# Batch 0's first key-value products in 32-column tiles, and one ScalarE instruction moved ahead of two copies

## The chip, the core and the metric

The kernel runs on one core of a Trainium2 chip. The metric is the device time of the whole program in microseconds (us); the figure quoted is the median of three runs. The engines are called PE (TensorE, matrix products), PEld (its weight loads), DVE (VectorE), ACT (ScalarE), POOL (GpSimd) and SP (SyncE, which here only issues DMA transfers). A line such as L444 is line 444 of the kernel. A "start" is counted in us from the beginning of the profiled span.

## What is computed

Attention with polynomial features, followed by a two-layer network with an exact GELU. Per batch (4) and head (4), with 1088 tokens of 32 numbers and two sketches S1, S2 of 8 rows each:

```
phi(x)[i, j] = (S1 x)[i] * (S2 x)[j]                 # 64 features a token
kv  = sum over tokens of phi(k) v^T ;  z = sum of phi(k)
x   = (phi(q) kv) / (phi(q) z + 1e-6)                # heads side by side: 4352 x 128
out = gelu(x @ w_in) @ w_out                         # 128 -> 2048 -> 128
```

The inputs moe_w_in and moe_w_out come as 64-bit floats, so each of their pieces is landed as pairs of 32-bit words and rounded to float32 by ACT, DVE and POOL before PE may use it.

## The kernel before

The bulk of the time is the two-layer network: for each chunk of 512 tokens, 16 products with w_in (`hidden`, L739), a GELU on ACT (L746) and products with w_out (L825, L876). The attention of batches 1 to 3 is woven into it. Batch 0 cannot be woven into anything: its attention stands at the head of the program, and the network begins when its first x is there. The change lies in that head, between 8.4 and 16 us of the span.

Every engine executes its instructions in the order of the program text (the last lines of the kernel, L1239 to L1245, fix that order by hand), and an instruction that waits holds up all behind it on its engine. The order of the text around the change:

- **PE**: the turn of the remainder keys (`key_turn_rem`, L347); `kv_first(kv_bank, 0, range(JC))`, the products of even heads for the first four token groups (L444); the sketches of the remainder keys (`key_features_rem`, L420); `kv_first(kv_bank, 0, range(JC, J))`, the other four groups; `kv_first(kv_bank, 1, parts=2)`, the odd heads; `kv_first_rem`, the remainder tokens (L450); the turn of the second query chunk (`query_turn(1)`, L347); the numerators of chunk 0 (`numerators_by_token`, L684, first into a bank called h_ps, then into one called o_ps); the first factor of chunk 1's query features (`expand_products(1, (0,))`, L569); the turn of the first half of x (L720); the second factor (L569); the turn of the second half (L712); the first hidden product in pieces (`first_hidden`, L755); then `hidden` (L739).
- **ACT**: the copy of the turned remainder keys (kT_rem, L349); the widening of v (L359); the copy of the remainder sketches (a_rem, L428); two copies for the query features of chunk 0 (A_sb, L575); the two copies of kv and z into kz_apart (L950), which is the moving operand of the numerators; the low words of w_in's first piece (`low_words`, L269); the exponents of that piece (L293); the copy of the turned second query chunk (qT, L954); one denominator (L705); the low words of w_in's second piece; half of x (L721); that piece's exponents (L293); a quarter of x (L714).
- **DVE**: two products of query features (q_pT, L580); the mantissas of w_in's first piece (bits_m, L301), which read the low words; the denominators and the division of the first half of x (L695, L697, L699); the signs (L306); the second half (L697, L699); the exponent and mantissa fields of w_in's second piece (L282, L287); its mantissas (L301); a quarter of x (L714).
- **POOL**: the features of the remainder keys (k_p_rem, L429), which `kv_first_rem` reads; two one-element fills that gate the loads of w_out on SP; the product that finishes w_in's first piece (L311).

A key-value product takes 128 tokens as its contraction, a token group's features as weights (64 of one head, or 32 with `parts=2`) and 33 columns of v with its column of ones as the moving operand. Each product is two records on PE. With 64 weights it takes a 128x64 tile of the array (written 128\*64 in the profile); with `parts=2` it takes a 128x32 tile (128\*32), and there are twice as many of them. Before the change the even heads use 128x64 tiles and the odd heads 128x32 tiles. The remainder products (L450), the sketches (L420) and the numerators (L684) are in 128x64 tiles throughout.

Of the kernel before, what the change touches and what calls it, by code (L numbers as in the profile page):

```python
# [16 lines left out]
def kernel(  # L17
# [26 lines left out]
    J = S // 128  # L44
    MAIN = J * 128
    REM = S - MAIN
    JC = 4
# [29 lines left out]
    def hidden_bank():  # L77
        return hps.tile([128, CW], FP, name="h_ps")

    def out_bank():  # L80
        return ops.tile([128, CW], FP, name="o_ps")
# [259 lines left out]
    def transposed(ps, name, srcs, copy, midway=lambda: None):  # L341

        n = len(srcs) * 128
        for i, s in enumerate(srcs):
            if 2 * i == len(srcs):
                midway()
            pe.transpose(ps[:, i * 128:(i + 1) * 128], in_=s, identity=ident)  # L347
        t = att.tile([128, n], FP, name=name, bufs=1 if name == "kT_rem" else 2)
        copy(out=t, in_=ps[:, :n])  # L349
        return t  # L350
# [10 lines left out]
    def widen_v_rem(b, copy=by_pool):  # L361
        if b:
            pool.memset(v_rem_aug[b], 0.0)
        rows = slice(b // 2 * REM, (b // 2 + 1) * REM)
        copy(out=v_rem_aug[b][rows, :, 0:D], in_=rem["v"][rows, b % 2])
# [51 lines left out]
    def key_features_rem(pair, ps, by_dve=True):  # L417

        for rows in (slice(0, 64), slice(64, 128)) if pair == 0 else (slice(0, 128),):
            pe.matmul(ps[rows, 384:448], lhsT=kT["rem"][:, rows], rhs=S12.rearrange("p h r -> p (h r)"), start=True, stop=True)  # L420
        k_p_rem[pair] = big.tile([128, H, R, R], FP, name=f"k_p_rem{pair}")
        ab = ps[:, 384:448].rearrange("p (h r) -> p h r", r=2 * R)
        a = att.tile([128, H, 2 * R], FP, name="a_rem")
        if by_dve:
            act.copy(out=a[:, :, 0:R], in_=ab[:, :, 0:R])
            dve.tensor_mul(**spread(k_p_rem[pair], a[:, :, 0:R], ab[:, :, R:2 * R]))
        else:
            act.copy(out=a, in_=ab)  # L428
            pool.tensor_mul(**spread(k_p_rem[pair], a[:, :, 0:R], a[:, :, R:2 * R]))  # L429
# [3 lines left out]
    def flat(features):  # L433
        return features.rearrange("p i j -> p (i j)")

    def kv_first(ps, r, tokens=range(J), parts=1):

        step = F // parts
        for i in tokens:
            for c in range(NP):  # L440
                for part in range(parts):
                    rows = slice(c * F + part * step, c * F + (part + 1) * step)
                    features = flat(k_p[0, r][:, i // JC, c * JC + i % JC])
                    pe.matmul(ps[rows, r * 2 * D:r * 2 * D + C], lhsT=features[:, part * step:(part + 1) * step],  # L444
                              rhs=v_aug[r][:, c, i, :C], start=(r == 0 and i == 0), stop=False, skip_group_check=True)
# [93 lines left out]
    def query_turn(n, copy=by_act):  # L539


        if n == 1:
            turned = transposed(hidden_bank(), "qT", [q_sb[1][:, h].rearrange("p j d -> p (j d)") for h in range(H)], copy)
            qT[n] = turned.rearrange("p (h j t) -> p h j t", h=H, j=JC)
            return
        qT[n] = att.tile([128, H, width[n] // 128, D], FP, name="qT" if n < NMAIN else "qT_rem")
        if n == 0:
            for c in range(NP):
                heads = slice(2 * c, 2 * c + 2)
                dve.transpose(out=qT[n][:, heads].rearrange("p h j t -> p h (j t)"),  # L550
                              in_=q_sb[n][:, heads].rearrange("p h j d -> p h (j d)"))
            return
        dve.transpose(out=qT[n].rearrange("p h j t -> p (h j t)"),
                      in_=q_sb[n].rearrange("p h j d -> p (h j d)") if n < NMAIN else q_rem.rearrange("p s b n d -> p (s b n d)"))
# [18 lines left out]
    def expand_copy(n, i):  # L573
        A[i] = att.tile([128, 2, CW // 2], FP, name="A_sb")
        act.copy(out=A[i][:, :, :width[n] // 2], in_=B_of[n, i][:, :, :width[n] // 2])  # L575
# [352 lines left out]
    kv_bank = out_bank()  # L928
# [1 line left out]
    widen_v(1, by_act, slice(0, JC))  # L930
    widen_v(1, by_pool, slice(JC, J))
    widen_v_rem(0, by_dve)
    kv_first(kv_bank, 0, range(JC))
    key_features_rem(0, second[1], by_dve=False)
    expand_copy(0, 0)
    w_in = [Rounding(w) for w in w_in_sb[:2]]
    w_in[0].fields()
    kv_first(kv_bank, 0, range(JC, J))
    expand_copy(0, 1)
    for i in range(2):  # L940
        expand_multiply(0, i)
# [3 lines left out]
    load_rest()  # L945
    late = []
    query_turn(1, lambda **a: late.append(a))
    for c in range(NP):
        rows = slice(c * F, (c + 1) * F)
        act.copy(out=kz_apart[rows, :, c], in_=kv_bank[rows, :128].rearrange("f (r x) -> f r x", r=2)[:, :, :C])  # L950
    w_in[0].low_words()
    w_in[0].exponents()
    w_in[0].mantissas()
    by_act(**late.pop())  # L954
# [1 line left out]
    parts = [range(2), range(2, JC)]  # L956
# [319 lines left out]
```

## Time and profile before

| what | value |
|---|---|
| median of three runs | 259.12 us (258.75 to 259.46) |
| the profiled execution: its own time | 259.21 us |
| the profiled execution: its span, first to last instruction | 257.4 us |
| busy share of PE, PEld, DVE, ACT, POOL | 98%, 52%, 59%, 45%, 64% |
| granted clock of TensorE | 1.0 |
| key-value products of batch 0 (L444) | 96 PE records: 32 in 128x64 tiles, 64 in 128x32 tiles, from 8.4 to 10.2 us |

The page of the profile gives busy time by engine, a picture of the span in 40 slices, and the chain of work that ended last. The timeline gives, in order of time, when a group of instructions starts, from its first start to its last end. PE's records overlap one another, so a group's length is not its cost: what counts is the distance from one start to the next.

### The profile page before, as it was taken

Reading aid. Unit: us, or ns where it says so; the run is one execution under the profiler, and the core shown is the slowest. Engines: PE = TensorE matmul, PEld = TensorE weight load, DVE = VectorE, ACT = ScalarE, POOL = GpSimd, SP = SyncE. Lnnn points to the kernel's source line nnn. Section 1 sums busy time; section 2 is a strip of 40 time slices with the busy share of each in tenths; the row PEclk is TensorE's granted clock in tenths of the full one; section 3 lists DMA queues with packets and bytes.
Section 4 is the critical chain, followed back from the end, with each engine's and each line's share of the span. In section 5 each row is a group of like instructions: output and inputs, shape, how many; then the busy total and the mean of one; then the engine's idle time right before and its main releaser. Section 6 shows DMA issues by size and latency. Waiting matters only on the chain.

```text
span 257.4 us, 5633 instructions
## 1 busy us (share of the span) xinstructions
PE 253.1 (98%) x2265; PEld 133.3 (52%) x2265; DVE 151.1 (59%) x314; ACT 115.1 (45%) x222; POOL 165.4 (64%) x175
## 2 busy tenths in 40 slices
PE   8999999999999999999999999999999999999995
PEld 4756444355444545444444455455544444445794
DVE  3886878969698987580178976399307000700330
ACT  3785767533535333533335332623444334433442
POOL 3414007799968788587758775787758777877300
PEclk9999999999999999999999999999999999999999
DMA  6699568610000101102000002000200200020020
GB/s 209 207 287 314 148 149 203 169 18 5 0 3 14 27 1 23 23 10 33 0 3 0 0 13 33 1 4 0 33 10 9 34 0 4 8 33 3 0 41 23
DMA packets 29082, 13.48 MB, mean 52 GB/s; under 512 B 21888, under 2 KB 27264, under 8 KB 29056
## 3 DMA queue, kind: packets, MB, share of 16 engines
q1 hardware_dynamic: 28624, 12.79, 20.2%
q8 instruction: 18, 0.29, 0.5%
q10 hardware_dynamic: 432, 0.33, 0.4%
q14 instruction: 8, 0.07, 0.1%
HBM read 10.88 MB, written 2.23 MB: 51 GB/s over the span
## 4 chain that ended last, share of the span: by engine, by line
PE 97%; ACT 1%; issue 0%
PE h_ps L739 45%; PE o_ps L825 33%; PE o_ps L876 5%; PE w_ps L873 3%; PE w_ps L455 1%; PE w_ps L603 1%; PE w_ps L658 1%; PE w_ps L908 1%; PE w_ps L569 1%; PE h_ps L755 1%; PE o_ps L444 1%; PE w_ps L994 1%; PE h_ps L347 1%; PE w_ps L684 0%; PE o_ps L396 0%; PE w_ps L485 0%
## 5 line engine op out<-in xcount | busy, mean ns | idle before, releaser
L739 PE MATMUL h_ps<-xT,w_in 128*64 128x512 f32 (+3 forms) x514 | 137.0, 576 | 0.0
L746 ACT ACTIVATE block<-h_ps 128x512 f32<-128x512 f32 (+1 forms) x128 | 73.2, 572 | 117.1 <-PE h_ps L739 115.2
L739 PEld LDWEIGHTS h_ps<-xT,w_in 128*64 128x64 f32 (+1 forms) x514 | 41.8, 142 | 30.7 <-issue 11.6
L825 PE MATMUL o_ps<-block,w_out 128*64 128x256 f32 x224 | 57.5, 379 | 0.0
L790 POOL TENSOR_TENSOR bits_low<-block 128x512 f32<-128x512 f32 x28 | 36.2, 1293 | 27.1 <-ACT block L746 27.1
L825 PEld LDWEIGHTS o_ps<-block,w_out 128*64 128x64 f32 x224 | 30.5, 137 | 38.1 <-issue 27.6
L791 POOL TENSOR_TENSOR bits_a<-block 128x512 f32<-128x512 f32 x28 | 35.8, 1278 | 11.7 <-ACT block L746 11.5
L840 DVE COPY sums<-o_ps 64x256 f32<-64x256 f32 x8 | 3.3, 417 | 60.6 <-PE o_ps L825 60.6
L792 POOL TENSOR_TENSOR bits_e<-bits_a,block 128x512 f32<-128x512 f32 x28 | 36.1, 1289 | 2.2
L793 POOL TENSOR_TENSOR bits_m<-block,bits_e 128x512 f32<-128x512 f32 x28 | 36.0, 1287 | 2.2
L825 PE MATMUL o_ps<-bits_a,small 128*64 128x256 f32 x112 | 28.8, 379 | 0.0
L825 PE MATMUL o_ps<-block,small 128*64 128x256 f32 x112 | 28.8, 379 | 0.0
L825 PE MATMUL o_ps<-bits_low,small 128*64 128x256 f32 x112 | 28.8, 379 | 0.0
L825 PE MATMUL o_ps<-bits_m,w_out 128*64 128x256 f32 x112 | 28.7, 379 | 0.0
L825 PEld LDWEIGHTS o_ps<-block,small 128*64 128x64 f32 x112 | 15.2, 137 | 17.9 <-issue 10.8
L825 PE MATMUL o_ps<-bits_e,small 128*64 128x256 f32 x112 | 17.0, 383 | 0.0
L876 PE MATMUL o_ps<-g,w_out 128*128 128x512 f32 (+1 forms) x34 | 16.5, 572 | 0.0
L825 PEld LDWEIGHTS o_ps<-bits_m,w_out 128*64 128x64 f32 x112 | 15.3, 137 | 0.0
L825 PEld LDWEIGHTS o_ps<-bits_a,small 128*64 128x64 f32 x112 | 15.2, 137 | 0.0
L825 PEld LDWEIGHTS o_ps<-bits_low,small 128*64 128x64 f32 x112 | 15.2, 137 | 0.0
L615 DVE STREAM_TRANSPOSE w_ps<-w_ps 128x512 f32<-128x512 f32 (+1 forms) x7 | 4.8, 687 | 17.1 <-ACT xT L669 12.7
L825 PEld LDWEIGHTS o_ps<-bits_e,small 128*64 128x64 f32 x112 | 7.6, 137 | 10.6 <-issue 8.8
(201 smaller groups left out, 302.9 us busy)
## 6 DMA issues: line engine op xcount, KB each, us to landing
block<-in_moe_w_in_dram SPq DMA_DIRECT2D x3, 512.0 KB, 9.6
block<-in_moe_w_out_dram SPq DMA_DIRECT2D x3, 512.0 KB, 9.7
k<-in_k_dram SPq DMA_DIRECT2D x12, 128.0 KB, 2.7
v<-in_v_dram SPq DMA_DIRECT2D x12, 128.0 KB, 2.9
q<-in_q_dram SPq DMA_DIRECT2D x24, 64.0 KB, 2.8
out_dram<-oT SPq DMA_DIRECT2D x21, 64.0 KB, 2.2
q_first<-in_q_dram SPq DMA_DIRECT2D x2, 256.0 KB, 3.9
v<-in_v_dram SPq DMA_DIRECT2D x2, 256.0 KB, 4.2
```

The costliest lines, as they stand in the source:

```text
L347: pe.transpose(ps[:, i * 128:(i + 1) * 128], in_=s, identity=ident)
L615: dve.transpose(out=tok, in_=ps[:, :, :H2])
L739: pe.matmul(ps[rows, :W], lhsT=w[:, rows], rhs=xT[n][:, :W], start=True, stop=True)
L746: act.activation(out=g_of[n, fi][:, :W], in_=ps[:, :W], func=ACT.Gelu)
L790: pool.tensor_sub(out=s[3], in0=a11, in1=a21)
L791: pool.tensor_add(out=s[1], in0=a21, in1=a22)
L792: pool.tensor_sub(out=s[2], in0=s[1], in1=a11)
L793: pool.tensor_sub(out=s[4], in0=a12, in1=s[2])
L825: pe.matmul(acc[n][bank][half * 64:(half + 1) * 64, col:col + HW], lhsT=fixed, rhs=moving, start=opens and e == 0 and name in "4715", stop ...
L840: dve.tensor_copy(out=N[lo, 0, one], in_=a0[lo, one])
L873: pe.matmul(o_of[n][i][:, :128], lhsT=g[:, i * 128:(i + 1) * 128], rhs=w_tile(w_out_sb, fi), start=first, stop=final)
L876: pe.matmul(o_of[n][:, cols], lhsT=w_tile(w_out_sb, fi), rhs=g[:, cols], start=first, stop=final)
```

## The change

Two edits. The even heads' key-value products of batch 0 are now issued in 128x32 tiles too (twice as many products of half the weights, into the same rows and columns of the bank). And the ACT instruction that takes the low words of w_in's first piece is issued ahead of the two copies into kz_apart instead of behind them. Nothing else in the text moves; no DMA is moved.

```diff
-    kv_first(kv_bank, 0, range(JC))
+    kv_first(kv_bank, 0, range(JC), parts=2)
     key_features_rem(0, second[1], by_dve=False)
     expand_copy(0, 0)
     w_in = [Rounding(w) for w in w_in_sb[:2]]
     w_in[0].fields()
-    kv_first(kv_bank, 0, range(JC, J))
+    kv_first(kv_bank, 0, range(JC, J), parts=2)
...
     query_turn(1, lambda **a: late.append(a))
+    w_in[0].low_words()
     for c in range(NP):
         rows = slice(c * F, (c + 1) * F)
         act.copy(out=kz_apart[rows, :, c], in_=kv_bank[rows, :128].rearrange("f (r x) -> f r x", r=2)[:, :, :C])
-    w_in[0].low_words()
     w_in[0].exponents()
     w_in[0].mantissas()
     by_act(**late.pop())
```

## The prediction

> **What bounds the kernel now.** I read the page first: shares of busy time, then the chain that ended last.
>
> ```profile
> span 257.4 us, 5633 instructions
> PE 253.1 (98%) x2265; PEld 133.3 (52%) x2265; DVE 151.1 (59%) x314; ACT 115.1 (45%) x222; POOL 165.4 (64%) x175
> ...
> PE 97%; ACT 1%; issue 0%
> ```
>
> PE bounds the program. From about 16 us to its last record it has no gap, so a shift of the head of the program reaches the end one to one, and nothing else can. What the change can be worth is the time that PE stands in the head. So I asked next what PE waits for there, and for the chain of waits from 8 to 16 us, where both edits lie.
>
> ```profile
> PE w_ps L569 <- ACT qT L954: 0.3, 1, 0.3
> ```
>
> ```profile
> 8.52 0.59 PE o_ps L444 x16
> 9.11 0.14 PE h_ps L420 x4
> 9.25 1.14 PE o_ps L444 x75
> 10.38 0.38 PE o_ps L450 x8
> ...
> 11.01 0.21 ACT kz_apart L950
> 11.22 0.02 issue
> 11.24 0.45 ACT bits_low L269
> 11.70 0.40 ACT bits_r L293
> 12.09 0.03 issue
> 12.12 0.60 ACT qT L954
> ...
> 12.76 0.69 PE w_ps L569 x16
> ```
>
> The reader is to see that the key-value products (L444) stand on this chain, that bits_low (the low words) stands on it too, and that PE then waits for qT: its last numerator record starts at 12.21, the next record at 12.76. Each edit takes something off this chain. The question is what lies beside it.
>
> **First edit: the tiles.** Record by record in the trace, the 128x64 form starts two records each 58 ns; a token group has four, 117 ns. The 128x32 form of the odd heads starts four records each 31 to 33 ns; a token group has eight, about 64 ns. Its 64 records run from 9.620 to 10.188. So eight groups of the even heads fall from 0.94 to 0.51 us of PE. But the tile changes more often: the last 64-column record (9.467) stands 153 ns ahead of the first 32-column one (9.620), where 52 would be usual, so a change of tile costs 0.10 us. Before there is one between L420 and L450 (64 to 32, and back at L450); after, L420 stands between two 32-column runs, which adds one to each side of it and takes away the one at 9.5: one more, 0.10. Net, 0.33 us less PE work up to L450.
>
> [...]
>
> What of that lies on the path? Two others end there.
> - L420 needs kT_rem from ACT, which ends at 8.82; PE answers an ACT copy after 0.05 (qT ends at 12.71, L569 starts at 12.76). So L420 cannot start before 8.87. The first four groups will be through by 8.73, with the change of tile 8.83. Now it starts at 8.94: 0.06 earlier, of which its second pair, after a stand, gives back some 0.02. Gain 0.04.
> - L450 needs k_p_rem from POOL, and that hangs on L420 through ACT's a_rem:
>
> ```profile
> 9.30 0.21 ACT L428 COPY a_rem<-h_ps 128x64 f32<-128x64 f32 x1 [0.17 <-PE h_ps L420]
> 9.59 0.63 POOL L429 TENSOR_TENSOR k_p_rem<-a_rem 128x256 f32<-128x256 f32 x1 [0.56 <-ACT a_rem L428]
> ```
>
> POOL ends at 10.22 and L450 starts at 10.31. After the change PE has finished the odd heads near 9.97 and could start L450 at 10.10; POOL ends at 10.18 and lets it at 10.27. So of 0.33 us, 0.29 become a stand of PE before L450, and 0.04 reach kz_apart. Bounds: nothing (L420 stays) to 0.06.
>
> **Second edit: the low words.** ACT's rows:
>
> ```profile
> 9.40 1.08 ACT L575 COPY A_sb<-w_ps 128x512 f32<-128x512 f32 x2
> 10.79 0.43 ACT L950 COPY kz_apart<-o_ps 64x66 f32<-64x66 f32 x2 [0.30 <-PE o_ps L450]
> 11.24 0.45 ACT L269 ACTIVATE bits_low<-small 128x256 f32<-128x256 uint32 x1
> 11.60 0.49 ACT L293 ACTIVATE bits_r<-bits_e,below 128x256 uint32<-128x256 uint32 x1
> ```
>
> Behind the two A_sb copies (starts 9.405 and 9.883, 0.478 apart) ACT could take its next instruction at 10.36, and kz_apart starts at 10.79: 0.43 us free. The low words cost ACT 0.36, start to start (11.24 to 11.60). They fit with 0.07 to spare, and the A_sb copies come with a_rem, so both ends of the gap move together. The words are there: DVE reads the same landed piece at 9.16. I cost the move at nothing for kz_apart; were the gap gone, it would cost at most 0.36. Behind the copies everything on ACT comes 0.36 earlier, with the first edit 0.40: exponents at 11.20, qT at 11.72 to 12.31, L569 at 12.36 instead of 12.76. PE is free for it: last numerator 12.17, plus a record and a change of tile, 12.32.
>
> **What is late next.** L569 is not the network. The first hidden product (L755) needs all of x, and x comes off DVE's chain:
>
> ```profile
> 11.73 0.43 DVE L301 SCALAR_TENSOR_TENSOR bits_m<-bits_a,bits_low 128x256 f32<-128x256 uint32 x1 [0.41 <-ACT bits_low L269]
> 12.07 0.16 DVE L695 TENSOR_SCALAR den_tok<-h_ps 128x8 f32<-128x8 f32 x1
> ```
>
> From L695 at 12.07 DVE runs without a pause to L282 at 13.82; ACT's exponents of the second piece wait for L282 and start at 14.26; the quarter of x behind them on ACT (L714) starts at 14.73 and ends at 15.00; PE takes the second half of L755 at 15.05. On PE's side that quarter was ready at 14.69. So two chains meet at 14.7, and the earlier L569 moves one of them alone. L695 waits for two things: bits_m ahead of it (11.73 and 0.34 behind) and the numerators' end (11.96, and 0.04 to DVE: 12.00). The second edit takes the first away: bits_m goes to 11.2. Then the numerators rule: 12.00, and with the 0.04 of the first edit 11.96. DVE's chain, and so the second half of L755, gains 0.11; the bounds are 0.07 (first edit worth nothing) and 0.13 (worth 0.06). L755's product of the weights on POOL (L311, 13.34 to 14.08) moves with DVE and is no later than L755's first half. The rest up to 16 us hangs on L755: the GELU at 15.80, and through it the third hidden product at 16.46.
>
> **Sum.** 0.04 through the remainder keys, 0.07 through bits_m: 0.11 us off the profiled execution's 259.21, 259.10. The median of the three runs is 259.12, 0.09 lower; taken off it, **259.0**. That is 0.04%, and I count anything within 0.3% (0.8 us) as not to be told from no change.
>
> **Rivals.**
> - *All of PE's stand comes off.* If the quarter of x on ACT followed PE instead of DVE's fields (PE has it 0.40 earlier), the gain is 0.40 plus the 0.07 that L755 stands at its second half: 258.7. For it: the chain of waits names ACT alone. Against: ACT's exponents start 0.04 after L282 ends.
> - *Nothing arrives.* L420 stays at 8.94, and L695 too, because the numerators end as they do and PE's word takes longer to reach DVE than 0.04: 259.1.
> [...]
> - *Narrow products pay by the record.* If the new records started at the 128x64 rate, 29 ns each, 64 of them would take 1.86 us instead of 0.94: L420 comes 0.47 later, L450 0.84 later, at 11.15, with kz_apart and all of x: 260.0, slower. It decides once a pair of records takes over some 40 ns, since beyond that POOL's cover is used up. Against it stand the odd heads' 64 records in 0.57 us.
>
> [...]
>
> **How the numbers follow.** Forecast 0.66 (259.0); nothing arrives 0.15 (259.1); all of the stand 0.10 (258.7); changes of tile 0.05 (259.2); by the record 0.04 (260.0). The range that leaves out no more than 2 in 10 must hold 258.7 to 259.2, and the medians of so few runs add about 0.3 to each side (three runs lay from 258.75 to 259.46): 258.4 to 259.5. Faster by over 0.3% is only the best case with a lucky median: 0.05. Slower by over 0.3% is the last rival and half a chance of something unseen: 0.06. Within 0.3%: 0.89.
>
> **What would show it.** Right: L420 starts near 8.87, and PE stands about 0.2 us before L450, which starts near 10.27; the low words start near 10.3 on ACT and kz_apart near 10.75; PE's wait for qT is gone; L695 starts near 11.96 and the second half of L755 near 14.94. Wrong: L450 earlier than POOL's end (then k_p_rem was not what it waits for); kz_apart later than 10.79 (then the low words did not fit); the quarter of x on ACT near 14.3 (the first rival). A granted clock below 1.0 anywhere would upset all of it; in this profile it is 1.0.

## The result, and the profile after

The changed kernel takes 259.84 us, the kernel before 259.23 us (medians of 22 runs each). The ratio is 1.0019, with a 95% interval from 1.0013 to 1.0026: slower by 0.5 us, where 0.1 us less was forecast; the median lies above the forecast range of 258.4 to 259.5. One of the 22 runs of the changed kernel was a slow one of 1500.25 us, which the ratio leaves out (the median of the other 21 is 259.82).

The chain that ended last, between 8 and 17 us of the changed kernel (start, length, what):

```profile
8.59 0.39 PE o_ps L444 x32
...
9.62 0.71 POOL k_p_rem L429
...
10.38 0.42 PE o_ps L450 x8
10.81 0.26 PE h_ps L347
11.07 0.51 issue
11.58 0.49 PE h_ps L347 x3
12.07 0.62 PE h_ps L684 x16
12.68 0.47 PE o_ps L684 x16
13.15 0.62 PE w_ps L569 x16
```

The low words and qT, which stood on the chain before, are off it. In their place there is a line that was not there: 0.51 us of "issue", inside L347. L347 is four equal records in a row that turn the second query chunk. The timeline of PE in the kernel before:

```profile
8.45 0.66 PE L444 MATMUL o_ps<-sums,k_p 128*64 128x33 f32 x16
...
10.67 0.66 PE L347 MATMUL h_ps<-ident,q_first 128*128 128x128 f32 x4
11.27 0.69 PE L684 MATMUL h_ps<-kz_apart,q_pT 128*64 128x66 f32 x16
...
15.60 2.96 PE L739 MATMUL h_ps<-xT,w_in 128*128 128x512 f32 x6
```

And in the changed one, with its weight loads and ACT behind it:

```profile
8.52 0.46 PE L444 MATMUL o_ps<-sums,k_p 128*32 128x33 f32 x32
...
10.38 0.42 PE L450 MATMUL o_ps<-v_rem_aug,k_p_rem 128*64 128x33 f32 x8
10.74 0.33 PE L347 MATMUL h_ps<-ident,q_first 128*128 128x128 f32 x1
11.58 0.49 PE L347 MATMUL h_ps<-ident,q_first 128*128 128x128 f32 x3 [0.51 <-issue]
12.00 0.69 PE L684 MATMUL h_ps<-kz_apart,q_pT 128*64 128x66 f32 x16
...
16.21 1.98 PE L739 MATMUL h_ps<-xT,w_in 128*128 128x512 f32 x4
```

```profile
10.74 0.20 PEld L347 LDWEIGHTS h_ps<-ident,q_first 128*128 128x128 f32 x2
11.58 0.25 PEld L347 LDWEIGHTS h_ps<-ident,q_first 128*128 128x128 f32 x2 [0.64 <-issue]
```

```profile
10.39 0.47 ACT L269 ACTIVATE bits_low<-small 128x256 f32<-128x256 uint32 x1
10.86 0.43 ACT L951 COPY kz_apart<-o_ps 64x66 f32<-64x66 f32 x2
11.31 0.51 ACT L293 ACTIVATE bits_r<-bits_e,below 128x256 uint32<-128x256 uint32 x1
12.10 0.59 ACT L954 COPY qT<-h_ps 128x512 f32<-128x512 f32 x1 [0.28 <-PE h_ps L347]
```

Everything ahead of 10.8 goes as forecast, to within 0.04 us once the 0.07 by which L444 starts later here is taken off: the low words fit ahead of kz_apart, and kz_apart is ready at 11.29. PE has issued two weight loads of L347 by 10.80 and issues the third only at 11.58. Nothing that the profile shows is waited for: the third turn needs q_first, whose loads had landed by 6.7. So the numerators (L684) start at 12.00, 0.7 us after their operand is ready, and all else follows: L569 at 13.08 instead of 12.76, the first whole hidden product (L739) at 16.21 instead of 15.60.

A measure that the start of the program disturbs less than the whole time is the distance from the first key-value product (L444) to the first whole hidden product (L739), called the stretch below: 15.60 - 8.45 = 7.15 us before, 16.21 - 8.52 = 7.69 after.

The page's part on DMA queues shows what I had passed over in the profile of before. The same line stands in both pages:

```profile
q8 instruction: 18, 0.29, 0.5%
```

18 transfers of 16 KB that carry instructions, for a program whose PE shows 4562 records (weight loads and products and waits): one transfer for each 253 records. The page does not say whose instructions they are; in the trace of before the 18 begin on average 256 PE records apart (the first at its record 189, the last at 4537), so they are taken to be PE's, and a transfer is called a fetch and what it brings a block below. The first of them begins at 8.80 in the kernel before, and at 9.18 in the changed one. That gave theory F: **PE ran out of instructions**. The change puts 64 more records ahead of L347 and lets PE come to them sooner. The rivals: W, that the moved low words delay something; T, that the more frequent change of tile costs more than 0.1 us.

### The profile page after: what moved, and what is told of

It reads as the page before. It is cut to its first block, busy times and chain, and to the rows that moved or that the text cites. A ratio compares the mean times of both kernels' runs of the same rounds, so it can differ in the third digit from the quotient of the medians.

```text
span 258.0 us, 5697 instructions
## 1 busy us (share of the span) xinstructions
PE 253.3 (98%) x2297; PEld 133.3 (52%) x2297; DVE 151.5 (59%) x314; ACT 115.0 (45%) x222; POOL 165.5 (64%) x175
## 4 chain that ended last, share of the span: by engine, by line
PE 97%; ACT 0%; issue 0%; POOL 0%; DVE 0%
PE h_ps L739 45%; PE o_ps L825 33%; PE o_ps L876 5%; PE w_ps L873 3%; PE w_ps L455 1%; PE w_ps L603 1%; PE w_ps L658 1%; PE w_ps L908 1%; PE h_ps L347 1%; PE w_ps L569 1%; PE h_ps L755 1%; PE w_ps L994 1%; PE w_ps L684 0%; POOL k_p_rem L429 0%; PE o_ps L396 0%
## 5 line engine op out<-in xcount | busy, mean ns | idle before, releaser
L739 PE MATMUL h_ps<-xT,w_in 128*64 128x512 f32 (+3 forms) x514 | 137.0, 576 | 0.0
L739 PEld LDWEIGHTS h_ps<-xT,w_in 128*64 128x64 f32 (+1 forms) x514 | 41.8, 142 | 30.6 <-issue 11.6
L791 POOL TENSOR_TENSOR bits_a<-block 128x512 f32<-128x512 f32 x28 | 35.8, 1278 | 11.6 <-ACT block L746 11.5
L825 PEld LDWEIGHTS o_ps<-block,small 128*64 128x64 f32 x112 | 15.2, 137 | 17.9 <-issue 10.8
```

The costliest lines, as they stand in the source:

```text
L739: pe.matmul(ps[rows, :W], lhsT=w[:, rows], rhs=xT[n][:, :W], start=True, stop=True)
L791: pool.tensor_add(out=s[1], in0=a21, in1=a22)
L825: pe.matmul(acc[n][bank][half * 64:(half + 1) * 64, col:col + HW], lhsT=fixed, rhs=moving, start=opens and e == 0 and name in "4715", stop ...
```

## The experiments

Ratios are to the kernel before, on the same chip, with 95% intervals.

**The first edit alone.** The low words are put back behind the copies.

> The first edit alone: the even heads' products in 128x32 tiles, the low words at their old place behind the copies into kz_apart. Theory F (PE runs out of instructions: the trace of the changed kernel has a hole in PE's issue from 10.80 to 11.58, between two of four identical turns in L347, after about 449 PE records, and the next 16 KB of PE's instructions were fetched only at 9.18): the hole stands at the same record, some 0.7 us long, and the time is 259.7 to 260.0, no better than with both edits. Rival W (the moved low words delay kz_apart or qT and with it PE): no hole, 259.1 to 259.2. Rival T (the more frequent change of tile drains PE): 259.8, but with the lost time at the changes of tile around L420 and L450 and none inside L347.

Measured: 259.76 us, ratio 1.0021 (1.0012 to 1.0030). The hole is there, behind the same record:

```profile
10.89 0.33 PE L347 MATMUL h_ps<-ident,q_first 128*128 128x128 f32 x1
12.03 0.49 PE L347 MATMUL h_ps<-ident,q_first 128*128 128x128 f32 x3 [0.81 <-issue]
```

W falls: without the moved words the loss is the same. The stretch is 7.91.

**The second edit alone.** `parts=2` is taken out of both calls for the even heads.

> The second edit alone: the low words ahead of the copies into kz_apart, the even heads' products in 128x64 tiles as before. Theory F: as many PE records ahead of L347 as before, so PE reaches its 449th record near 12.2, after the fetch is in; no hole; L569 near 12.4 instead of 12.76, the first division near 12.00, and 259.1 to 259.2, 0.05 to 0.15 below the kernel before, as the prediction's second step had it. Rival W: 259.8. Rival T: 259.1 to 259.2 as F.

Measured: 259.27 us, ratio 0.9999 (0.9990 to 1.0007). No hole, and PE's wait for qT is gone. The stretch is 7.04, 0.11 less than before; a second profile of this kernel gave 7.04 again, and a second one of the kernel before 7.14.

```profile
10.66 0.47 ACT L269 ACTIVATE bits_low<-small 128x256 f32<-128x256 uint32 x1
11.09 0.43 ACT L951 COPY kz_apart<-o_ps 64x66 f32<-64x66 f32 x2
...
14.51 0.51 ACT L293 ACTIVATE bits_r<-bits_e,below 128x256 uint32<-128x256 uint32 x1 [0.33 <-DVE bits_e L282]
14.92 0.24 ACT L714 COPY xT<-o_ps 128x128 f32<-128x128 f32 x1
```

The low words fit into ACT's gap, and the quarter of x (L714) waits behind DVE's fields (L282), as the prediction had it. The gain shows in the profiles; in the time it is too small for these runs.

**Half of the tiles.** Both edits, but the last four groups of the even heads stay in 128x64 tiles: 32 records more than before instead of 64.

```diff
-    kv_first(kv_bank, 0, range(JC, J), parts=2)
+    kv_first(kv_bank, 0, range(JC, J))
```

> Both edits, but only the first four token groups of the even heads in 128x32 tiles; the other four stay in 128x64 tiles. That is 32 PE records more ahead of L347 than before where the full change has 64 more. Theory F: the 449th record is now one of the numerators (L684, first bank) at about 11.3 to 11.7, near the time at which the next instructions arrive (11.58 in the changed kernel): a hole of at most 0.3 us, 259.1 to 259.4, less than half the loss for half the records. Rival T: there is a change of tile on one side of L420 only, half the loss: 259.5. Rival W: 259.8.

Measured: 259.25 us, ratio 0.9999 (0.9990 to 1.0008). The stretch is 7.30. The hole is 0.3 us and has moved into the numerators, 16 records of the load queue further on in the text:

```profile
11.12 0.48 PEld L684 LDWEIGHTS h_ps<-kz_apart,q_pT 128*64 128x64 f32 x13 [0.18 <-ACT kz_apart L951]
11.80 0.14 PEld L684 LDWEIGHTS h_ps<-kz_apart,q_pT 128*64 128x64 f32 x2 [0.19 <-issue]
```

Counted in the trace, the last weight-load record ahead of the hole is the 230th of PE's load queue (weight loads and waits together; with the products some 449 PE records) here, in the changed kernel and with the first edit alone. The line is another, the count is the same. T, which ties the loss to the changes of tile, has no place for that. Its expectation of half the loss rested on a miscount: from the first L444 to L450 this kernel enters a new tile form four times (32, 64, 32, 64 columns), as the changed kernel does, where the kernel before does so three times; yet its time is that of the kernel before, and so T is out. The hole ends 2.3 to 2.6 us after the fetch began (9.18 and 11.58 changed, 9.45 and 12.03 with the first edit alone, here 9.54 and 11.80). In the kernel before, PE comes to its 230th record at 12.09, 3.3 us after the fetch began, and does not stop there.

**More records in the head, first try.** One of the two idle products at the start is replaced by 32 small ones.

```diff
-    keep_busy(2, bank, 448)
+    keep_busy(1, bank, 448)
+    for i in range(32):
+        at = i % 4 * 32
+        noughts = [nc.const_aps.tensor(0.0, [128, m], FP) for m in (32, 24)]
+        pe.matmul(bank[at:at + 32, :24], lhsT=noughts[0], rhs=noughts[1], start=True, stop=True)
```

> The changed kernel, with one of the two idle products on noughts at the very start (L908) replaced by 32 small ones of 32 weights and 24 columns: 126 to 128 PE records more in the head, where PE only waits for the first loads. Nothing else is altered. Theory F: the end of the loaded instructions now falls some 128 records earlier in the text, among the odd heads' products near 9.5, and the fetch of the next block is asked for about 2 us earlier, near 5.6 instead of 7.7; no hole in L347, and 259.1 to 259.3. Rivals T and W: 259.8 as the changed kernel. [...]

Measured: 260.83 us, ratio 1.0064 (1.0050 to 1.0078), a miss as a time. L347 runs through (11.67, four records in one group), and the stretch is 7.15. But the trace's first record of granted clock 1.0 begins at 7.92 us (at 5.5 in the profile of before, 5.1 to 6.8 in the others with the old head), and the first key-value product starts at 9.34 instead of 8.45. The head was changed in more than its number of records, so its time tells nothing of the hole. A pause of 0.33 us stands in L444 instead, behind the 229th load record (one short of the 230 of the other runs; why was not followed up), and ends 2.8 us after the fetch began. The times at which a fetch is "asked for" (5.6 and 7.7) are a guess of mine, which no trace shows: what shows is the beginning of the transfer, 9.18 in the changed kernel and near 7.9 here.

**A head as busy as before.** 40 products of 32 weights and 96 columns replace both idle products: 160 records instead of 8.

> The changed kernel with both idle products at the start (L908) replaced by 40 on noughts, of 32 weights and 96 columns, four tiles side by side: 160 PE records instead of 8 in the same 3.3 us, so that the array stays as busy there and the clock should come as early. Theory F (in the changed kernel, with the first edit alone and with half the tiles, the hole stands behind the 230th record of PE's load queue, whatever line that is, and ends 2.3 to 2.6 us after the fetch of PE's next 16 KB began): the boundary moves 152 records ahead in the text, to the sketches near 9.0, and the fetch is asked for in the head, long before; no hole, from the first key-value product (L444) to the first whole hidden product (L739) 7.0 to 7.1 us, against 7.15 before and 7.69 changed, and 259.0 to 259.2 if the clock comes at 5 to 6.7 as elsewhere. Theory T (changes of tile) or any other cost in the tiles themselves: 7.69 and 259.8.

Measured: 259.62 us, ratio 1.0013 (1.0004 to 1.0021). That a busy head brings the clock as early was a guess from the run before (7.92 against 5.5), and so was the fetch "asked for" in the head; the trace has only the transfer. The hole in L347 is gone, and the fetch begins at 6.82:

```profile
11.06 0.66 PE L347 MATMUL h_ps<-ident,q_first 128*128 128x128 f32 x4
```

The stretch is 7.12, just above the 7.0 to 7.1 expected. The 230th load record lies in the second run of L444 (9.74), not in the sketches as expected; behind it there is a pause of 0.14 us, where 0.01 is usual; it ends 3.1 us after the fetch began, so whether the block is its cause is not shown, and PE waits for POOL at L450 anyway. At the end of the next block, between the two loads of L720, there is one of 0.1, and it ends 2.3 us after that block's fetch began (11.29). The time is 0.5 above what F gave, and the next run but one shows the greater part of why.

**A whole block more.** 66 products of 58 columns: 264 records instead of 8, 256 more.

> As the run with 160 head records, but with 66 products of 58 columns: 264 records instead of 8, which moves the text by 256 records against the blocks of 256 that the fetches bring, a whole block. Theory F: the next boundary now falls on the same instruction of L347 as in the changed kernel, with its fetch asked for at the same place; the hole is back, 0.5 to 1.1 us long, L444 to L739 7.6 to 7.9, and 259.7 to 260.0. A theory in which the head itself (more small products, a busier array) cures the hole: no hole, 7.05 and 259.1.

Measured: 260.80 us, ratio 1.0053 (1.0040 to 1.0067). The hole is back on the same instruction:

```profile
11.53 0.20 PEld L347 LDWEIGHTS h_ps<-ident,q_first 128*128 128x128 f32 x2
12.40 0.25 PEld L347 LDWEIGHTS h_ps<-ident,q_first 128*128 128x128 f32 x2 [0.67 <-issue]
```

Now the last load record ahead of it is the 358th, 128 later, with 128 products that belong to them: 256 records, one block. The block's fetch begins at 10.03 and the hole ends at 12.40, 2.4 us later. The program's one block more is on the page, too; every other kernel here has 18:

```profile
q8 instruction: 19, 0.31, 0.5%
```

The stretch is 7.64. The time is 0.8 above the expected range; in this profile the first key-value product starts only at 9.39, behind a wait of L569 for the first qT that the other heads do not show. What this head does to the start beyond that was not followed up.

**The head's own price.** The kernel before with the head of 160 records.

> The kernel before, with the head of 160 records: a control for the head. Theory F: no hole before and none now; L444 to L739 7.1 to 7.2 and 259.1 to 259.3, so that the difference to the changed kernel with the same head is what the change is worth without the hole, 0.05 to 0.15 us. If the head costs or brings time by itself (the clock), this run shows it.

Measured: 259.66 us, ratio 1.0012 (1.0003 to 1.0021). So this head costs about 0.3 us by itself, and with it the changed kernel (1.0013) and the kernel before (1.0012) cannot be told apart: where the hole is cured, the loss of the change is gone. A gain of 0.1 is below what these intervals resolve. In the profile of this run the record of granted clock 1.0 begins at 4.0 us, and PE then has a pause of 0.6 for v, so its stretch (7.93) is not used.

**Less in transfer beside the fetch.**

```diff
-    load_w_in(1, gated=True)
...
     key_features_rem(0, second[1], by_dve=False)
+    load_w_in(1, gated=True)
```

> The changed kernel with the load of w_in's second piece issued some 1.2 us later (its gate on POOL behind the features of the remainder keys), so that 256 KB less are in transfer while PE's instructions are fetched near 9.2. Theory F with the fetch slowed by the data: the hole ends earlier, 2.0 us or less after the fetch began or with an earlier fetch, and the time falls to 259.3 to 259.6. Theory F with a fetch that takes its time whatever else is in transfer: the same hole, 259.7 to 260.0.

Measured: 259.89 us, ratio 1.0021 (1.0011 to 1.0030). The hole is no shorter (10.91 to 11.88 in the load records), the fetch begins at 9.28 and the hole ends 2.6 us later. From 9.3 to 11.2 us this trace shows no other DMA packet at all, where the changed kernel has the load's packets from about 10.0 on; so this load is not what makes the fetch slow.

**As many records as before, head untouched.**

```diff
-    kv_first(kv_bank, 0, range(JC, J), parts=2)
```

> The changed kernel with the even heads' products of the last four token groups left out (so kv lacks them): 64 PE records less ahead of L347, as many as the kernel before has there, all with the head untouched. PE stands before L450 for POOL's features in the changed kernel already, so the work itself lies beside the path. Theory F (the hole stands behind the 230th record of the load queue and ends 2.3 to 2.6 us after the fetch began): PE comes to that record only among the numerators of the second bank, near 11.9, when the block is in: no hole, or under 0.2 us; L444 to L739 7.0 to 7.15 instead of 7.69, and 259.0 to 259.3. If the tiles or the changes of tile cost the 0.6 us, at most their share in the left-out groups goes: 259.5 to 259.8.

Measured: 259.06 us, ratio 0.9988 (0.9978 to 0.9999).

```profile
10.34 0.43 PE L450 MATMUL o_ps<-v_rem_aug,k_p_rem 128*64 128x33 f32 x8 [0.31 <-POOL small L187]
10.70 0.65 PE L347 MATMUL h_ps<-ident,q_first 128*128 128x128 f32 x4
11.30 0.69 PE L684 MATMUL h_ps<-kz_apart,q_pT 128*64 128x66 f32 x16
```

L347 is whole again, and the stretch is 6.97. L450 starts nearly where it starts in the changed kernel (1.81 us after the first L444, 1.87 there), since it waits for POOL in both; so the work left out is not what was gained. Of the 0.72 us that the stretch lost, 0.06 came ahead of L450 and the rest behind it, where the hole had been. The 230th load record comes at 12.11, 3.2 us after the fetch began. As the products that are left out are part of the result, this kernel is a control and no candidate.

**Second profiles.**

> The kernel before once more, for a second profile: no hole, L444 to L739 7.1 to 7.2 as in the first one, and the 230th record of the load queue reached 0.5 us or more after the end of the fetch's usual 2.3 to 2.6 us.

> The changed kernel once more, for a second profile: the hole at the same record in L347, 0.5 to 1.1 us, and L444 to L739 7.5 to 7.9.

> The second edit alone once more, for a second profile: no hole, L444 to L739 7.0 to 7.1, some 0.1 below the kernel before, PE's wait for qT gone and L755's second half waiting for the quarter of x on ACT.

Measured: no hole, 7.14; a hole from 10.99 to 11.80 behind the 230th load record, 7.64; no hole, 7.04. In the kernel before the 230th record comes 3.2 us after the fetch began, in the changed one the hole ends 2.6 us after it.

## Why the prediction was wrong

The sum, 0.11 us less, failed at one step: "Net, 0.33 us less PE work up to L450", after which only kT_rem, POOL and ACT were asked whether they held PE up. The step counted what the new records take on the array and left out that each is an instruction that has to be there: the sum has no term for the arrival of PE's instructions, which puts it at nothing, and it cost some 0.7 us of the stretch (7.69 with the hole, 6.97 in the kernel with the part left out). 64 more of them ahead of L347 moved the end of the loaded block from the second bank of numerators (12.1 in the kernel before) to L347 (10.8), and the block behind it came at 11.6. The stand of PE that the prediction had placed before L450 is there (0.26 us of idle load queue) and harmless, as forecast; behind it came a second one, the hole of 0.8 us, and that one had no cover: "L695 starts near 11.96" became 12.73, since the numerators that it waits for started at 12.00 instead of 11.2.

The other steps, each against the start of L444 (0.07 later in the profile of the changed kernel than before):
- *A token group costs 64 ns in 128x32 tiles.* Right: the 96 records of twelve groups start from 9.21 to 10.04, 0.83 us, where 0.77 follows. The rival by which narrow products pay by the record is out (it had priced itself a little low: 1.86 less 0.94 is 0.92 us for L450, not 0.84). These records start 8 to 9 ns apart on average, where that rival took 29.
- *A change of tile costs 0.10.* Right: from L420's last record (9.056) to the next 128x32 one (9.208) are 0.15, where 0.05 is usual. The 259.2 to which 0.05 was given, also the upper end of 258.7 to 259.2, supposes a dearer change of tile, which no run shows.
- *L420 at 8.87, L450 near 10.27.* 8.94 and 10.38; with the 0.07 taken off, right, and 0.04 late, since POOL's features took 0.71 us instead of 0.63 in this profile.
- *The low words cost kz_apart nothing.* Right: in the kernel with the second edit alone they start at 10.66 and kz_apart at 11.09, 0.05 after the end of L450, as before.
- *DVE's chain and the quarter of x hold the second half of L755; 0.07 through bits_m and 0.04 through the remainder keys.* Right in kind and somewhat small in size: the second edit alone shortens the stretch by 0.11; the kernel with the part left out, which has both gains and no hole, by 0.18.

So the plan of the change was read rightly and its price was not. None of the rivals that I had named was this one. The time did stay within 0.3% of the kernel before, to which 0.89 was given, but as a loss for a reason that the forecast did not have; with 22 runs that loss can be told from no change. The row that could have raised the question was in the page of before: instructions arrive by DMA, 18 times. With the 2.6 us that were measured only afterwards, PE's 230th load record comes 0.7 us or so after the block can be used in the trace of before (8.80 + 2.6 = 11.4 against 12.09). The edit asked PE to be there 1.3 us sooner.

Two measurements give the size of the block: 18 transfers of 16 KB on the page, and the hole a whole 256 records further on when 256 are put ahead (behind the 358th load record instead of the 230th). At a block's end PE stood 0.3 to 1.1 us from one weight load to the next in six kernels of this study.

What stays open: what the fetch is triggered by, why PE gets its instructions only 2.3 to 2.8 us after the transfer's record begins when that record is 0.9 to 1.4 us long, and what the small products in the head cost. No complete kernel here beats the kernel before by more than can be measured; the second edit alone is equal to it.

## What to carry to other kernels

Splitting the products into narrower tiles brought a token group from 117 to 64 ns of PE here, and doubled its instructions. In a dense opening, count PE's records up to the next instruction transfer, and ask whether PE will be there before it: the number of transfers is on the page of before, their times and the record count are in its trace. A hole marked "issue" between equal instructions, at a record count that stays the same when the text moves, was here a block that had not come. The word "issue" alone does not tell that: the load queue has 0.4 us of it ahead of L720 in the kernel before, too.

## What the runs showed of the hardware that was not expected

- Transfers of 16 KB that carry instructions, 18 on the page of before, begin on average 256 PE records apart in its trace and are taken to be PE's; the holes stood behind the 230th record of its load queue (the 229th in one run) and, with 256 records put ahead, behind the 358th. PE went on 2.3 to 2.8 us after such a transfer began, in seven profiles with a hole.
- A load of 256 KB issued beside the transfer or 1.2 us later made no difference to that (2.4 and 2.6 us), though in the second case no other packet was in transfer for 1.9 us of it.
- The first record of granted clock 1.0 began between 4.0 and 7.9 us in 14 profiles, and the first key-value product between 7.97 and 9.39; within the ten that share the old head, between 5.1 and 6.8 and between 8.34 and 8.80. What sets it was not tested.
